# The weights' sums for the seven-product units on VectorE alone, without GpSimd

## The chip, the cores and the metric

One core of a Trainium2 chip. The metric is the device time of one execution in microseconds (us); the kernel before takes 732.95 us (median of 3 runs, 732.93 to 733.94). TensorE multiplies matrices (PE is its matmul, PEld its weight load), VectorE (DVE) and ScalarE (ACT) work element by element, GpSimd (POOL) does so too and issues the indirect gathers, SyncE (SP) issues most other transfers. Each engine takes its instructions in order; an instruction that waits for another engine holds up all that stand behind it on its own.

## The reference

Block-sparse attention and then a layer-normed feed-forward block, on q, k, v of 4 batches x 8 heads x 768 positions x 64. Cut to what matters:

```python
scores = scale * q @ k.T                      # per head; blocks of 32 positions
scores = where(mask, scores, -1e9)            # neighbours, first and last block, 3 sampled blocks
attn = softmax(scores) ; x = attn @ v         # x: (4, 768, 512)
xn = (x - mu) / sqrt(var + 1e-6) * g_ln
out = x + maximum(xn @ w_ch1, 0) @ w_ch2      # w_ch1: 512 x 2048, w_ch2: 2048 x 512
```

## The kernel before

The 768 positions of a batch are 6 tiles of 128, and 24 tiles in all. Attention goes in *visits*: a visit computes the scores of 4 or 8 heads of one tile (`scores`, L242), their maximum on VectorE (`biggest`, L286), softmax on ScalarE (`softmax`, L299), turns the weights with eight transposes on TensorE (`turn_pe`, L307), evicts those on ScalarE (`turn_act`, L310), and multiplies by the values (`attn_v`, L326), which VectorE scales (`evict`, L368 to L374). The finished tile is normed, and its transposed halves xt are made: GpSimd subtracts the high half from xn (`norm_5`, L423), and SyncE's queue turns both halves with transposing DMAs (L431, L432).

Two tiles are a unit of the feed-forward block. Weights and activations are held as pairs of fp16 tensors, a high and a low half; a product is three matmuls. Units 0 and 1 multiply plainly (`ffn_items`: L459 up, L468 and L471 the two halves after relu, L484 down, L435 the residual add, L439 the store). From unit 2 on (`wino_items`) the down product of two tiles and a 2 x 2 split of the second weight (B11, B12, B21, B22) is done with seven block products in place of eight: L564 is the up product, L571 its eviction by ScalarE into three buffers in turn (`con_s` the first), L572 to L574 the sums of activations, L583 and L584 their two halves, L589 the seven products. Three PSUM banks take the up products in turn, so TensorE can't begin the fourth group before L571 has emptied the first.

The seven products need four sums of weight blocks, S1 to S4, once. `combos` makes a list of them: the eight column slices go in four pairs, and for each pair 18 steps, each over 128 x 512 elements:

| step | engine before | what |
|---|---|---|
| 1, 2, 3 | GpSimd, VectorE, GpSimd | t = B12 + B22, high and low halves (L526) |
| 4, 5 | ScalarE, VectorE | S1 = -t, rounded to a high half (L521), and the rest as the low half (L522) |
| 6, 7, 8 | VectorE, GpSimd, VectorE | t = B11 - B12 (L526) |
| 9, 10 | ScalarE, VectorE | S3 |
| 11, 12 | GpSimd, VectorE | t = B22 - t (L526) |
| 13, 14 | ScalarE, VectorE | S2 |
| 15, 16 | GpSimd, VectorE | t = B21 - t (L526) |
| 17, 18 | ScalarE, VectorE | S4 |

t is one half of `con_s`, so two pairs run side by side; the list takes step 1 of one pair, step 1 of the other, step 2 of one, and so on, and then the same for the other two pairs: 72 entries, of which 20 are GpSimd's, 36 VectorE's and 16 ScalarE's.

From visit 13 on the list is emptied: 15 entries a visit, spread over the visit's other tasks (the gathers of values and the load of the next keys, `turn`, `norms`, and TensorE's share of the feed-forward block between them). So visits 13 to 16 take 15 each and visit 17 the last 12. Visit 16 begins in the second pair of pairs with the end of step 5, and visit 17 with step 13. Within a visit each engine's order is: `scores`, `biggest`, `attn_v` and `evict` of the visit before, `softmax`, and then the tasks. In visit 16 GpSimd's order is the store, three gathers and a sum, the fourth gather and a sum, L423, and a copy for the keys; SyncE's is L431, L432, then the keys and values of the visit after next (L190, L221, twelve of L196).

Scores start at 137.4 us in visit 13, 151.5 in visit 14, 165.3 in visit 15, and as the rows below show in visits 16, 17 and 18.

```python
for lo in range(0, NW, 2):                     # in combos
    t = con_s[:, 512 * (lo // 2 % 2) :][:, 0:512].rearrange("p (f e) -> p f e", e=256)
...
h = len(fns) // 4
return [f for k in (0, 2 * h) for x in zip(fns[k : k + h], fns[k + h : k + 2 * h]) for f in x]
...
if s == visits[NPV].job.visits[-1].i + 1:      # in the loop over visits, s = 13
    late.extend(combos())
k = min(15, len(late))
```

Of the kernel before, what the change touches and what calls it, by code (L numbers as in the profile page):

```python
# [14 lines left out]
ALU = mybir.AluOpType  # L15
# [10 lines left out]
def sparse_attention_moe(  # L26
# [19 lines left out]
    nc = tc.nc  # L46
# [460 lines left out]
    def block(w, r, c):  # L507
        return w[:, r * NW : r * NW + NW, 256 * c : 256 * c + 256]

    B11, B12, B21, B22 = ([block(w, r, c) for w in (w2h, w2l)] for r in range(2) for c in range(2))  # L510
# [6 lines left out]
    def combos():  # L517
        fns = []

        def rounded(t, dst, c, sign=1.0):  # L520
            fns.append(lambda: nc.scalar.activation(dst[0][:, c], t, AF.Copy, scale=sign))  # L521
            fns.append(lambda: nc.vector.scalar_tensor_tensor(out=dst[1][:, c], in0=t, scalar=sign, in1=dst[0][:, c],  # L522
                                                              op0=ALU.mult, op1=ALU.subtract))

        def op(eng, o, a, b, fn=ALU.add):
            fns.append(lambda: eng.tensor_tensor(out=o, in0=a, in1=b, op=fn))  # L526

        for lo in range(0, NW, 2):
            c = slice(lo, lo + 2)
            t = con_s[:, 512 * (lo // 2 % 2) :][:, 0:512].rearrange("p (f e) -> p f e", e=256)  # L530
            v, g = nc.vector, nc.gpsimd
            op(g, t, B12[0][:, c], B22[0][:, c])
            op(v, t, t, B12[1][:, c])
            op(g, t, t, B22[1][:, c])
            rounded(t, S1, c, -1.0)
            op(v, t, B11[0][:, c], B12[0][:, c], ALU.subtract)
            op(g, t, t, B11[1][:, c])
            op(v, t, t, B12[1][:, c], ALU.subtract)
            rounded(t, S3, c)
            for p, q in ((B22, S2), (B21, S4)):  # L540
                op(g, t, p[0][:, c], t, ALU.subtract)
                op(v, t, t, p[1][:, c])
                rounded(t, q, c)
        h = len(fns) // 4
        return [f for k in (0, 2 * h) for x in zip(fns[k : k + h], fns[k + h : k + 2 * h]) for f in x]
# [255 lines left out]
    def node(eng, cost, prio, fn, *args, after=(), dma=None, alloc=None, free=None, at=0.0, port=False):  # L801
        k = SimpleNamespace(eng=eng, cost=cost, prio=prio, fn=fn, args=args, dma=dma, alloc=alloc, free=free,
                            at=at, todo=0, next=[], start=None, must=True, port=port)
        for x in after:
            if x is not None:
                k.todo += 1
                x.next.append(k)
        nodes.append(k)
        return k
# [9 lines left out]
    for i in range(16):  # L819
# [15 lines left out]
        if LOWS[i] == "e":  # L835
            LO[i] = []
            for k in range(2):
                p = node("PE", 1.0, pr, low_pe, i, k, after=[HI[i]], alloc=(i, k))
# [133 lines left out]
    while left:  # L972
# [12 lines left out]
        while events and events[0][0] <= now + 1e-9:  # L985
            fn, args = heapq.heappop(events)[2:]
# [77 lines left out]
    while s < NV + LAG + 2 or queue or nextu < len(units):  # L1064
# [6 lines left out]
        if pvi:  # L1071
            t = pvi.tile
# [49 lines left out]
        if s == visits[NPV].job.visits[-1].i + 1:  # L1122
            late.extend(combos())
# [78 lines left out]
```

## Time and profile before

| | us |
|---|---|
| median of 3 runs | 732.95 |
| profiled execution | 739.73 |
| its span | 738.0 |
| TensorE busy in it | 696.5 (94%) |
| VectorE busy | 472.2 (64%) |
| GpSimd busy | 273.4 (37%) |

Time rows read: start in us, duration in us, engine, line, operation, output<-input, shapes and count; in brackets the idle time of the engine just before, and what ended it. Several instructions of one kind in a row are merged: "1.28 ... x2" is two in 1.28 us. An idle TensorE also shows as slow instructions, where a group waits between its members. The releaser named is the last event of those that the instruction waited for, by inference. "L242" is line 242 of the kernel printed above.

### The profile page before, as it was taken

The numbers are of one execution on the slowest core, as the hardware profiler recorded it, in microseconds if no ns is written. First come the engines' busy times: TensorE is split into PE (matmuls) and PEld (weight loads), VectorE is DVE, ScalarE is ACT, GpSimd is POOL, SyncE is SP. The second block draws the span as 40 slices with busy tenths as digits, with TensorE's granted clock in tenths as the row PEclk, the third lists the DMA queues.
The fourth block names the chain that finished last, engine by engine and source line by source line (L and its number), as shares of the span: only waits on it lengthen the run. The fifth ranks groups of instructions, "written<-read, shape, count | busy, mean of one in ns | idle before, by whom it ended". The sixth has DMA issues, their size and how long they took to land.

```text
span 738.0 us, 24907 instructions
## 1 busy us (share of the span) xinstructions
PE 696.5 (94%) x10258; PEld 553.1 (75%) x10258; DVE 472.2 (64%) x945; ACT 350.1 (47%) x668; POOL 273.4 (37%) x321
## 2 busy tenths in 40 slices
PE   2889988999879999999999999999999999999997
PEld 1466764675467888878888887788888878788886
DVE  4879986476577567558458468458458368448271
ACT  1577753453346455436446355336346355445150
POOL 3832732576655112435244113545353112520000
PEclk9999999999999999999999999999999999999999
DMA  8993861565367544677867554676678644750100
GB/s 332 411 391 142 289 201 56 151 167 161 90 192 219 159 163 139 170 188 217 197 189 226 176 161 117 181 237 190 175 212 193 198 141 119 179 163 16 44 1 30
DMA packets 127954, 128.83 MB, mean 175 GB/s; under 512 B 83681, under 2 KB 107745, under 8 KB 125153
## 3 DMA queue, kind: packets, MB, share of 16 engines
q1 hardware_dynamic: 117024, 92.09, 42.3%
q0 software_dynamic: 10528, 35.07, 15.2%
q8 instruction: 81, 1.33, 0.8%
q14 instruction: 33, 0.26, 0.1%
q10 hardware_dynamic: 288, 0.08, 0.0%
HBM read 115.40 MB, written 6.29 MB: 165 GB/s over the span
## 4 chain that ended last, share of the span: by engine, by line
PE 75%; DVE 10%; DMA 5%; issue 4%; SPq 2%; POOL 2%; ACT 0%; DVEq 0%; ACTq 0%; POOLq 0%
PE pu L564 26%; PE pd_X L589 10%; PE pd_Z L589 10%; PE ps L242 7%; PE pv L326 7%; PE pt L307 6%; PE pd_Y L589 3%; PE pu L459 3%; PE pd L484 2%; SPq L196 2%; DMA w2h<-w 2%; DVE st L286 1%; DVE con L526 1%; POOL con L526 1%; DMA ks<-kTh 1%
## 5 line engine op out<-in xcount | busy, mean ns | idle before, releaser
L227 POOL DMA_INDIRECT vs<-v,rows x152 | 161.4, 1062 | 219.3 <-PE pv L326 174.0
L564 PE MATMUL pu<-xt,w1h 128*128 128x256 f16 x1280 | 173.0, 273 | 3.0 <-DMA ks<-kTh 2.2
L299 ACT ACTIVATE p<-ps,st 128x256 f32<-128x256 f32 (+1 forms) x208 | 85.8, 490 | 119.3 <-DVE rs L368 44.6
L564 PEld LDWEIGHTS <-w1h 128*128 128x128 f16 x1280 | 123.9, 98 | 19.6 <-issue 3.4
L310 ACT COPY pt<-pt 128x512 f32<-128x512 f32 x120 | 61.4, 561 | 78.3 <-PE pt L307 31.6
L564 PE MATMUL pu<-xt,w1l 128*128 128x256 f16 x640 | 96.4, 273 | 0.0
L589 PEld LDWEIGHTS <-h 128*128 128x128 f16 x840 | 81.2, 98 | 11.8 <-issue 1.6
L286 DVE TENSOR_REDUCE st<-ps 128x4 f32<-128x1024 f32 (+1 forms) x60 | 68.9, 1149 | 32.2 <-PE ps L242 32.1
L326 PEld LDWEIGHTS pv<-vs,pt 128*32 128x32 f32 x3584 | 54.5, 109 | 31.5 <-issue 23.6
L242 PE MATMUL ps<-ks,q 64*32 64x256 f32 (+3 forms) x1952 | 71.4, 369 | 2.4 <-DMA ks<-kTh 1.3
L307 PE MATMUL pt<-id_sb,p 128*128 128x128 f32 x448 | 63.7, 281 | 10.1 <-ACT p L299 6.2
L326 PE MATMUL pv<-vs,pt 128*32 128x65 f32 x3584 | 65.8, 221 | 4.3 <-issue 3.5
L435 DVE SCALAR_TENSOR_TENSOR x<-pd_Z,x 128x256 f32<-128x256 f32 x40 | 16.1, 422 | 82.3 <-PE pd_Z L589 56.2
L564 PEld LDWEIGHTS <-w1l 128*128 128x128 f16 x640 | 62.3, 98 | 7.6
L307 PEld LDWEIGHTS pt<-id_sb,p 128*128 128x128 f32 x448 | 51.1, 143 | 18.6 <-ACT p L299 10.3
L242 PEld LDWEIGHTS ps<-ks,q 64*32 64x32 f32 x1952 | 33.4, 107 | 24.0 <-issue 15.3
L589 PEld LDWEIGHTS <-stg 128*128 128x128 f16 x420 | 40.4, 98 | 6.5 <-issue 0.9
L423 POOL TENSOR_TENSOR xl<-xn,xh 128x512 f16<-128x512 f32 x21 | 24.4, 1162 | 41.9 <-ACT xh L400 41.6
L439 POOL DMA_DIRECT2D out<-x x20 | 11.7, 587 | 73.6 <-DVE x L435 67.7
L484 PE MATMUL pd<-w2h,h 128*128 128x512 f16 x128 | 38.4, 379 | 0.0
L572 DVE TENSOR_TENSOR con<-con 128x256 f32<-128x256 f32 x30 | 12.8, 427 | 38.5 <-ACT con L571 33.9
L459 PE MATMUL pu<-xt,w1h 128*128 128x256 f16 x256 | 35.4, 273 | 0.0
(181 smaller groups left out, 1171.5 us busy)
## 6 DMA issues: line engine op xcount, KB each, us to landing
vs<-vN SPq DMA_DIRECT2D x35, 520.0 KB
ks<-kNh SPq DMA_DIRECT2D x32, 512.0 KB
ks<-kTh SPq DMA_DIRECT2D x384, 32.0 KB
q<-qT SPq DMA_DIRECT2D x24, 256.0 KB
w2h<-w SPq DMA_DIRECT2D x5, 1024.0 KB
out<-x POOLq DMA_DIRECT2D x20, 256.0 KB
vs<-vD SPq DMA_DIRECT2D x6, 780.0 KB
ks<-kTh SPq DMA_DIRECT2D x12, 384.0 KB
```

What stands on the lines that cost most here:

```text
L227: nc.gpsimd.indirect_dma_start(out=vj.buf[:, vj.far + gg, :], out_offset=None, in_=src, in_offset=bass.IndirectOffsetOnAxis(ap=rows[:, i : ...
L242: nc.tensor.matmul(ps[32 * part : 32 * part + 32, col : col + n], lhs[64 * row : 64 * row + 64], rhs[64 * row : 64 * row + 64], start=True ...
L286: nc.vector.tensor_reduce(out=st[:, 0:n], in_=seen(vi), axis=AX.X, op=ALU.max, negate=True)
L299: nc.scalar.activation(p_s[:, h * w : (h + 1) * w], seen(vi)[:, h, :], AF.Exp, bias=vi.st[:, 4 + h : 5 + h], scale=0.125)
L307: nc.tensor.transpose(pt[:, k - lo, :], p_s[:, k * P : (k + 1) * P], id_sb)
L310: nc.scalar.copy(pt_s[:, lo:hi, :], vi.pt.pop(lo)[:, 0 : hi - lo, :])
L326: nc.tensor.matmul(pv[32 * row : 32 * row + 32, 65 * col : 65 * col + 65], pt[:, ch, 32 * row : 32 * row + 32], vj.buf[:, vv, lo : lo + 65 ...
L423: nc.gpsimd.tensor_sub(xl_s[t.n % 2], xn_s, xh_s[t.n % 2])
L459: nc.tensor.matmul(ph[:, j * n : (j + 1) * n], w[:, ct, fs], x[:, ct, 0:n], start=m == 0, stop=m == 3 * CT - 1, skip_group_check=True)
L484: nc.tensor.matmul(po, x[:, f, ts], w[:, f, :], start=m + f == 0, stop=m == 2 and f == FT - 1)
L564: nc.tensor.matmul(ph[:, j * 256 : j * 256 + 256], w[:, ct, f * P : (f + 1) * P], x[:, ct, :], start=m == 0, stop=m == 3 * CT - 1, skip_gr ...
L589: nc.tensor.matmul(o, HW[j][x][:, i, :], t[w][:, j, :], start=first and m + j == 0, stop=False, skip_group_check=True)
```

## The change

The 20 sums that GpSimd made (steps 1, 3, 7, 11 and 15 of each pair) become VectorE's, in the same place of the list. Operands, buffers, the number of entries and where they are put in the visits stay as they are. ScalarE's 16 roundings stay.

```diff
--- before.py
+++ after.py
@@ -522,24 +522,23 @@
             fns.append(lambda: nc.vector.scalar_tensor_tensor(out=dst[1][:, c], in0=t, scalar=sign, in1=dst[0][:, c],
                                                               op0=ALU.mult, op1=ALU.subtract))
 
-        def op(eng, o, a, b, fn=ALU.add):
-            fns.append(lambda: eng.tensor_tensor(out=o, in0=a, in1=b, op=fn))
+        def op(o, a, b, fn=ALU.add):
+            fns.append(lambda: nc.vector.tensor_tensor(out=o, in0=a, in1=b, op=fn))
 
         for lo in range(0, NW, 2):
             c = slice(lo, lo + 2)
             t = con_s[:, 512 * (lo // 2 % 2) :][:, 0:512].rearrange("p (f e) -> p f e", e=256)
-            v, g = nc.vector, nc.gpsimd
-            op(g, t, B12[0][:, c], B22[0][:, c])
-            op(v, t, t, B12[1][:, c])
-            op(g, t, t, B22[1][:, c])
+            op(t, B12[0][:, c], B22[0][:, c])
+            op(t, t, B12[1][:, c])
+            op(t, t, B22[1][:, c])
             rounded(t, S1, c, -1.0)
-            op(v, t, B11[0][:, c], B12[0][:, c], ALU.subtract)
-            op(g, t, t, B11[1][:, c])
-            op(v, t, t, B12[1][:, c], ALU.subtract)
+            op(t, B11[0][:, c], B12[0][:, c], ALU.subtract)
+            op(t, t, B11[1][:, c])
+            op(t, t, B12[1][:, c], ALU.subtract)
             rounded(t, S3, c)
             for p, q in ((B22, S2), (B21, S4)):
-                op(g, t, p[0][:, c], t, ALU.subtract)
-                op(v, t, t, p[1][:, c])
+                op(t, p[0][:, c], t, ALU.subtract)
+                op(t, t, p[1][:, c])
                 rounded(t, q, c)
         h = len(fns) // 4
         return [f for k in (0, 2 * h) for x in zip(fns[k : k + h], fns[k + h : k + 2 * h]) for f in x]
```

## Rows read from the trace of the kernel before

**Rows 1.** The page's part 4: chain that ended last, shares of the span

```profile
PE 75%; DVE 10%; DMA 5%; issue 4%; SPq 2%; POOL 2%; ACT 0%; DVEq 0%; ACTq 0%; POOLq 0%
```

**Rows 2.** Busy time by stretch: engines busy (operations), granted clock, DMA share, GB/s

```profile
135.00:215.00 80.00, 72.84 (x905) 49.62 (x903) 49.16 (x78) 30.91 (x66) 52.46 (x50) 0.98 0.59 167
205.00:210.00 5.00, 4.21 (x26) 3.61 (x27) 2.64 (x7) 2.60 (x6) 2.47 (x4) 0.66 0.71 187
240.00:720.00 480.00, 476.47 (x7079) 401.12 (x7078) 294.85 (x649) 229.41 (x438) 148.00 (x161) 1.00 0.57 159
```

**Rows 3.** TensorE's timeline, 130 to 225 us: start, duration, [idle before <-releaser]

```profile
145.57 1.04 PE L307 MATMUL pt<-id_sb,p 128*128 128x128 f32 x8
...
158.57 1.53 PE L307 MATMUL pt<-id_sb,p 128*128 128x128 f32 x8 [0.29 <-issue]
...
180.97 1.09 PE L242 MATMUL ps<-ks,q 64*32 64x256 f32 x32
...
187.37 1.53 PE L307 MATMUL pt<-id_sb,p 128*128 128x128 f32 x8 [1.12 <-ACT p L299]
...
192.28 1.09 PE L242 MATMUL ps<-ks,q 64*32 64x256 f32 x32
...
200.89 1.03 PE L564 MATMUL pu<-xt,w1h 128*128 128x256 f16 x8 [0.79 <-DMA xt<-xl]
...
205.79 1.97 PE L307 MATMUL pt<-id_sb,p 128*128 128x128 f32 x8 [3.21 <-issue]
...
207.55 1.40 PE L564 MATMUL pu<-xt,w1h 128*128 128x256 f16 x6
...
216.00 0.38 PE L564 MATMUL pu<-xt,w1h 128*128 128x256 f16 x2 [2.25 <-DMA ks<-kTh]
...
216.31 1.34 PE L242 MATMUL ps<-ks,q 64*32 64x256 f32 x32
```

**Rows 4.** Groups by line, 134 to 222 us: busy us, mean ns | idle before

```profile
L526 DVE TENSOR_TENSOR con<-con,w2l 128x512 f32<-128x512 f32 x16 | 16.0, 1024 | 13.3 <-POOL con L526 13.3
...
L526 POOL TENSOR_TENSOR con<-w2h,con 128x512 f32<-128x512 f16 x8 | 10.6, 1345 | 5.6 <-DVE vs L522 4.0 <-ACT pt L310 1.6
```

**Rows 5.** VectorE's timeline, same stretch and columns

```profile
178.53 2.57 DVE L526 TENSOR_TENSOR con<-con,w2l 128x512 f32<-128x512 f32 x2 [1.43 <-POOL con L526]
...
182.82 0.98 DVE L522 SCALAR_TENSOR_TENSOR ks<-con,ks 128x512 f16<-128x512 f32 x1 [1.72 <-ACT ks L521]
...
185.32 1.22 DVE L286 TENSOR_REDUCE st<-ps 128x4 f32<-128x1024 f32 x1
...
188.60 1.28 DVE L526 TENSOR_TENSOR con<-w2h 128x512 f32<-128x512 f16 x2
...
194.60 0.69 DVE L526 TENSOR_TENSOR con<-con,w2l 128x512 f32<-128x512 f32 x1 [4.72 <-POOL con L526]
...
203.58 1.21 DVE L286 TENSOR_REDUCE st<-ps 128x4 f32<-128x1024 f32 x1
...
207.38 1.29 DVE L522 SCALAR_TENSOR_TENSOR vs<-con,vs 128x512 f16<-128x512 f32 x2 [1.54 <-issue]
```

**Rows 6.** GpSimd's timeline, same stretch and columns

```profile
192.43 0.95 POOL L227 DMA_INDIRECT vs<-v,rows  x1 [0.30 <-issue]
...
193.40 1.16 POOL L526 TENSOR_TENSOR con<-con,w2l 128x512 f32<-128x512 f32 x1
...
197.25 1.16 POOL L423 TENSOR_TENSOR xl<-xn,xh 128x512 f16<-128x512 f32 x1
...
220.38 1.65 POOL L227 DMA_INDIRECT vs<-v,rows  x1 [0.30 <-issue]
```

**Rows 7.** ScalarE's timeline, same stretch and columns

```profile
215.34 0.61 ACT L571 ACTIVATE con<-pu 128x512 f32<-128x512 f32 x1
```

**Rows 8.** SyncE's DMA queue, same columns: duration is that of the issue

```profile
198.44 1.19 SPq L432 DMA_TRANSPOSE xt<-xl  x1
...
200.93 6.68 SPq L196 DMA_DIRECT2D ks<-kTh  x12
```

## The prediction

> **What bounds the kernel now.** I read four views in this order: the chain of waits, the busy time by stretch, the timeline of the stretch in which the sums run, and the timelines of the queues behind it. The chain is three quarters TensorE [rows 1], and from 240 to 720 us TensorE is busy 476.47 of 480 us at the full granted clock [rows 2]: what is saved or lost before 240 moves the rest as a block. The sums run between about 134 and 215 us (visits 13 to 17). From 135 to 215 TensorE loses 80 - 72.84 = 7.2 us, while VectorE is busy only 49.16 of 80 [rows 2]. So I ask of each TensorE gap there which engine ended it, and whether the sums stood in that engine's queue.
>
> They do. VectorE's 16 low-half sums wait 13.3 us for GpSimd and take 1024 ns each, because they run beside GpSimd's own sums, which take 1345 ns [rows 4]. The same VectorE pair takes 1.28 us for two when GpSimd is not summing (188.60), but 2.57 when it is (178.53) [rows 5]. In order behind it stands the maximum of the scores (L286): in visit 17 the scores were done by 193.4 [rows 3], yet L286 starts at 203.58 [rows 5], since VectorE sat 4.72 us for a GpSimd sum that stood behind gathers [rows 5, 6]. TensorE's transposes need softmax, and start 2.1 to 2.2 us after L286 starts [rows 3, 5].
>
> **The gaps, and what each costs.** A normal group of eight transposes takes 1.04 us [rows 3].
> - G1, 158.57: 0.29 idle and 0.49 slow (1.53 against 1.04).
> - G2, 187.37: 1.12 idle, 0.49 slow.
> - G3, 200.89: 0.79 idle for xt, whose low half GpSimd (L423) makes behind two sums [rows 3, 6].
> - G4, 205.79: 3.21 idle; then transposes 0.93 slow and the next matmuls some 0.6 slow (six in 1.40; eight take 1.03 at 200.89, so six some 0.8), as the granted clock fell to 0.66 of full in that stretch, so part of it at the lower of its two levels (1.2 against 2.4 GHz) [rows 2, 3]. In all 4.7.
> - G5, 216.00: 2.25 idle, then scores 0.25 slow (1.34 against 1.09). The view names a key load, but TensorE starts just as ScalarE's eviction at L571 ends (215.34 + 0.61) [rows 3, 7]; ScalarE came to it only after steps 17, which waited for sums.
>
> **The change part by part.** It removes 20 GpSimd sums, adds 20 to VectorE, and moves nothing else; the order on each engine stays. *Price of a moved sum:* 0.64 us, half of the pair of 1.28, since the steps of two column blocks alternate. Bounds: below, no gain beyond 0.64 is shown; above, 1.29, half of the disturbed pair of 2.57 [rows 5]. I take 0.64: the cause of the 1.29, a GpSimd sum alongside, goes. So VectorE gets 20 x 0.64 = 12.8 us, and loses 16 x (1.024 - 0.64) = 6.1 of disturbance and 13.3 of waiting [rows 4]. It would be busy 49.2 - 6.1 + 12.8 = 56 of 80: it fits. *GpSimd* loses some 20 x 1.3 = 26 us; nothing waits for that but its gathers, stores and L423, which come earlier.
>
> What the same queues give, visit by visit:
> - Visit 14: two more sums (step 7, 1.3) stand ahead of L286, but waits and disturbance go, on average (13.3 + 6.1) / 5 = 3.9 a visit. More than G1 asks for; it gives 0.7 (estimate: the idle and most of the slow part).
> - Visit 15 to 16: VectorE waited 1.43 before 178.53 and 1.72 before 182.82, and was disturbed by 1.29 in the pair and 0.3 in step 5 [rows 5]: 4.7 less. Steps 1 and 3 add 4 x 0.64 = 2.6. L286 moves from 185.32 to about 183.2, after the scores of visit 16 (done by 182.1 [rows 3], 0.7 earlier by G1). G2's idle goes: 1.1; the slow part I leave.
> - Visit 17: from L286 of visit 16 to 188.60 is 3.3 [rows 5], so step 6 starts at 186.5; steps 6, 7, 8, 10, 11 and 12 are 12 operations, 7.7, and a hand-over to ScalarE some 0.2. L286 comes at 194.4, 9 us earlier; transposes could start at 196.6. TensorE gets there at (205.79 - 3.21) - 0.7 - 1.1 - 0.8 = 200.0: cover 3.4. G4 gives 4.7.
> - G3: L423 stands behind four gathers and the store; that chain starts when VectorE ends the residual add just ahead of 188.60 [rows 5], which moves by 2.1, and loses the two sums of 1.16 [rows 6] and pauses of some 0.2: L423 from 197.25 to 192.6. G3 gives 0.8.
> - G5: after L286 of visit 17 step 14 follows in 3.8 (before, 203.58 to 207.38, by the softmax), then steps 14, 15, 16 and a residual add, 7 x 0.64 = 4.5; ScalarE's step 17, two evictions of transposes and L571 are four operations, at L571's 0.61 [rows 7] another 2.4: 194.4 + 3.8 + 4.5 + 2.4 = 205.1. TensorE wants it at (216.00 - 2.25) - 7.3 = 206.4. Cover 1.3, the thinnest; G5 gives 2.5.
>
> Sum: 0.7 + 1.1 + 0.8 + 4.7 + 2.5 = 9.8 us.
>
> **What is late next.** The key loads of visit 18 leave SyncE behind L432 (198.44), which waits for L423; they are issued by 207.6 [rows 8]. No row shows when they land; the nearest is the transpose DMA: 198.44 to TensorE's start at 200.89, 2.45 [rows 3, 8]. With L423 4.6 earlier they are usable at 207.6 - 4.6 + 2.45 = 205.5. TensorE wants them at 216.31 - 9.6 = 206.7. Cover 1.2, so this costs nothing, but only just.
>
> The profiled execution took 739.73 (span 738.0), 6.8 over the median 732.95; I take the 9.8 from either: span 728.2, median 723.2.
>
> **The rivals.**
> *A, GpSimd's queue gains less than I think.* A gather that starts at 220.38 takes 1.65 instead of 0.95 [rows 6]. If a busier VectorE does that to all four, L423 loses 2.8, the keys come at 208.3 and TensorE waits 1.6: 724.8. If L423 does not move at all, keys come at 207.6 + 2.45 = 210.1, 3.4 late, and the clock may fall again for the 1.5 it cost in G4: gain 9.8 - 4.9, 728.0. For it: the cover is 1.2. Against: the gathers at 192 take 0.95 [rows 6], though VectorE was idle then.
> The Trainium skill ("SBUF — State Buffer", section "Who interferes with whom") says that a VectorE instruction with two SBUF inputs contends with a GpSimd instruction that reads SBUF, and infers that descriptor generation, which needs the write interface, is left alone by tensor_tensor. By that the gathers would stay at 0.95 and A would cost nothing; the 1.65 row leaves it open.
> *B, VectorE becomes the engine waited for.* At 1.29 a sum, L286 of visit 16 comes at 183.2 + 4 x 0.65 = 185.8: G2 stays and grows by 0.5. L286 of visit 17 comes at 199.6 and costs little; L571 is 10 x 0.65 = 6.5 later, 211.6, so TensorE goes on 4.4 earlier than now, and 0.25 of slow scores goes: gain about 4.6, 728.3.
> The Trainium skill ("Perfetto Trace Analysis", section "Optimizing Scalar/DVE Operations") says that where VectorE is saturated, moving work to GpSimd may make sense. That speaks for the kernel as it is, with B's result; VectorE's 49.16 of 80 says that the condition is not met.
> *C, slower: a moved sum waits out a gather.* Place: visits 16 and 17, where gathers and sums now run together. The fall comes back when L571 is 10.9 us later than I have it (205.1 to 216.0), ten sums before it: from 0.64 + 1.09 = 1.73 us a sum. With a gather of 0.95 and a half of a second, a sum takes 2.0; L571 is 13.6 later, 218.7: 2.7 slower, 735.6. For it: VectorE's sums did double beside GpSimd's. Against: gathers take 0.95 to 1.65 each and there are four a visit, not one for each sum.
> *D, no change:* the gain is given back by key loads later. Against: after 240 TensorE waits 3.5 us in all [rows 2].
>
> **How the numbers follow.** My forecast 0.65 (721.5 to 724.5: the slow halves of G1 and G2 add up to 0.6, the thin covers take 1.3), A 0.15, B 0.08, D 0.05, C 0.07. Forecast, A and B are faster: 0.88; same 0.05; slower 0.07; 0.2% (1.5 us) is about what a measurement of this kernel can tell. The range reaches from 720.5 (less by the 0.6, by 0.5 of gaps before 215 that I did not count, by as much again just after 216, and by the 1.0 that runs of the kernel before differ) to 728.5 (A and B in), leaving C and D out.
>
> **What would show it.** Right: all 40 sums (L526) on VectorE, near 0.64 each; no VectorE wait for GpSimd; L286 of visit 17 near 194; no granted clock below full at 205; L423 near 193; TensorE over 79 of 80 busy in the stretch; the stretch after 240 alike, moved by 10 us. Wrong: TensorE waiting for key loads at visit 18 (A), or L286 and ScalarE's evictions still late with VectorE near full (B, C).

## The result, and the profile after

The changed kernel takes 721.97 us (median of 5; before 732.95, median of 5): ratio 0.9845, 95% interval 0.9825 to 0.9865, 11.0 us faster. The forecast was 723.2 with 9.8 us. One execution of the 5 took 1415.92 us, with matmuls of 442 ns where the others of this study have 273, and is left out of the ratio; it was the one that was profiled, so the trace below is of the same kernel, run once more (719.21 us).

The opening stage differs from execution to execution by several us: the scores of visit 13 begin at 137.40 in the trace of before, at 131.90 in this one, and between 131.5 and 140.2 in the others. The stretch behind differs too: from the scores of visit 19 to the end it is 507.2 us in the trace of before, 503.4 in this one, and 502.7 to 508.1 in the others. So the time of one trace is not compared with that of another; traces are laid beside one another from visit to visit, from the start of one visit's scores to the next. All in us:

| kernel | 13 | 14 | 15 | 16 | 17 | 18 | 13 to 18 |
|---|---|---|---|---|---|---|---|
| before | 14.05 | 13.82 | 15.70 | 11.31 | 24.03 | 14.51 | 93.42 |
| changed | 13.63 | 12.87 | 15.70 | 9.53 | 15.75 | 14.59 | 82.07 |

The 0.42 of visit 13 is of that one execution of before: kernels with the old sums in visit 13 have 13.62 too (the last pairs, below). The rest, 10.9 us, is the change, about what the medians give (11.0), and it sits where the gaps were: 0.95 in visit 14 (G1), 1.78 in visit 16 (G2), 8.28 in visit 17 (G3 to G5).

Busy time by stretch (columns as in rows 2), first before, from the scores of visit 13 to those of visit 18, then the changed kernel over the same work and after it:

```profile
137.40:216.31 78.91, 70.75 (x893) 48.44 (x892) 49.70 (x79) 30.67 (x64) 50.23 (x48) 0.98 0.59 169
```

```profile
131.90:199.38 67.48, 67.11 (x892) 47.50 (x891) 56.79 (x99) 30.82 (x64) 26.98 (x28) 1.00 0.62 176
226.00:700.00 474.00, 472.65 (x7054) 399.10 (x7053) 290.52 (x642) 226.56 (x432) 147.48 (x161) 1.00 0.58 162
```

TensorE does the same matmuls in 67.48 us instead of 78.91 (busy 70.75 before, the slow ones among them, and 67.11 now), and its granted clock is 1.00, against 0.98 before. VectorE has 7.1 us more to do (the forecast: 12.8 - 6.1 = 6.7) in a stretch that is 11 us shorter, so it is busy 84% of it and not 63%.

TensorE's timeline of the changed kernel (columns as in rows 3; lines behind the edit have a number one lower than before, and in the runs with added lines one that is some higher):

```profile
145.53 1.09 PE L242 MATMUL ps<-ks,q 64*32 64x256 f32 x32
...
152.19 1.04 PE L307 MATMUL pt<-id_sb,p 128*128 128x128 f32 x8
...
158.40 1.09 PE L242 MATMUL ps<-ks,q 64*32 64x256 f32 x32
...
174.10 1.09 PE L242 MATMUL ps<-ks,q 64*32 64x256 f32 x32
...
179.21 1.04 PE L307 MATMUL pt<-id_sb,p 128*128 128x128 f32 x8
...
183.63 1.09 PE L242 MATMUL ps<-ks,q 64*32 64x256 f32 x32
...
190.69 1.04 PE L563 MATMUL pu<-xt,w1h 128*128 128x256 f16 x8
...
192.22 1.04 PE L307 MATMUL pt<-id_sb,p 128*128 128x128 f32 x8
...
199.08 0.38 PE L563 MATMUL pu<-xt,w1h 128*128 128x256 f16 x2 [0.37 <-ACT con L570]
199.38 1.37 PE L242 MATMUL ps<-ks,q 64*32 64x256 f32 x32
...
207.93 1.53 PE L307 MATMUL pt<-id_sb,p 128*128 128x128 f32 x8 [0.78 <-ACT p L299]
```

Of the gaps, G1 to G4 have no successor: the transposes of visits 14, 16 and 17 (152.19, 179.21, 192.22) take the normal 1.04 without a wait, and so does the up product that waited for xt (190.69). Of G5 0.37 is left (199.08), the scores behind it are slow as before, and the wait of visit 18 (207.93) is one that the kernel before has too (0.73 us at 224.77 in its trace). VectorE's, GpSimd's and ScalarE's timelines of the changed kernel:

```profile
180.87 2.49 DVE L526 TENSOR_TENSOR con<-con,w2l 128x512 f32<-128x512 f32 x4
...
185.87 2.69 DVE L526 TENSOR_TENSOR con<-con,w2l 128x512 f32<-128x512 f32 x2
188.49 1.21 DVE L286 TENSOR_REDUCE st<-ps 128x4 f32<-128x1024 f32 x1
```

```profile
180.95 1.46 POOL L227 DMA_INDIRECT vs<-v,rows  x1 [0.30 <-issue]
182.72 1.47 POOL L227 DMA_INDIRECT vs<-v,rows  x1 [0.30 <-issue]
...
186.84 1.16 POOL L423 TENSOR_TENSOR xl<-xn,xh 128x512 f16<-128x512 f32 x1
```

```profile
198.42 0.61 ACT L570 ACTIVATE con<-pu 128x512 f32<-128x512 f32 x1
```

Four sums in a row take 2.49 us (180.87), 0.62 each, and no sum waits for another engine. Counted from the scores of visit 13, L286 of visit 17 comes at 56.6 instead of 66.2 [rows 5], L423 at 54.9 instead of 59.9 [rows 6], L571 (now L570) at 66.5 instead of 77.9 [rows 7]; the 0.42 of visit 13 is in each of these differences. But the pair at 185.87 takes 2.69, beside L423, which reads too; and the two gathers at 180.95 and 182.72, beside the sums, take 1.46 and not 0.95: what rival A named does occur.

The sums by form, 128 to 215 us of the changed kernel (columns as in rows 4):

```profile
L526 DVE TENSOR_TENSOR con<-con,w2l 128x512 f32<-128x512 f32 x24 | 17.3, 770 | 0.0
...
L526 DVE TENSOR_TENSOR con<-w2h,con 128x512 f32<-128x512 f16 x8 | 5.4, 706 | 0.0
...
L526 DVE TENSOR_TENSOR con<-w2h 128x512 f32<-128x512 f16 x8 | 5.1, 682 | 0.0
```

Against 1024 ns and a wait of 13.3 us [rows 4], the mean is 0.68 to 0.77 us and the wait is none.

### The profile page after: what moved, and what is told of

Read it like the earlier page. It is cut to its first block, busy times and chain, and to the rows that moved or that the text cites. A ratio compares the mean times of both kernels' runs of the same rounds, so it can differ in the third digit from the quotient of the medians.

```text
span 1414.2 us, 24904 instructions
## 1 busy us (share of the span) xinstructions
PE 1397.7 (99%) x10258; PEld 846.3 (60%) x10258; DVE 478.4 (34%) x965; ACT 359.6 (25%) x668; POOL 238.3 (17%) x301
## 4 chain that ended last, share of the span: by engine, by line
PE 99%; DMA 1%; ACT 0%; DVE 0%; DVEq 0%; issue 0%
PE pu L563 32%; PE pd_X L588 12%; PE pd_Z L588 12%; PE ps L242 8%; PE pv L326 8%; PE pt L307 7%; PE pu L459 6%; PE pd L484 6%; PE pd_Y L588 4%; PE pw L716 2%; DMA id_sb<-eye 1%; PE pw L717 1%; PE idle L796 0%; PE px L408 0%; PE px L416 0%; ACT w1l L722 0%
## 5 line engine op out<-in xcount | busy, mean ns | idle before, releaser
L563 PE MATMUL pu<-xt,w1h 128*128 128x256 f16 x1280 | 337.5, 442 | 0.0
L563 PEld LDWEIGHTS <-w1h 128*128 128x128 f16 x1280 | 185.1, 146 | 108.8 <-issue 4.7
L563 PE MATMUL pu<-xt,w1l 128*128 128x256 f16 x640 | 183.2, 447 | 0.0
L588 PEld LDWEIGHTS <-h 128*128 128x128 f16 x840 | 124.4, 149 | 69.1 <-issue 2.2
L286 DVE TENSOR_REDUCE st<-ps 128x4 f32<-128x1024 f32 (+1 forms) x60 | 69.2, 1153 | 210.9 <-PE ps L242 210.8
L326 PEld LDWEIGHTS pv<-vs,pt 128*32 128x32 f32 x3584 | 96.2, 147 | 54.4 <-issue 35.2
L307 PE MATMUL pt<-id_sb,p 128*128 128x128 f32 x448 | 117.4, 446 | 1.1 <-ACT p L299 1.1
L242 PE MATMUL ps<-ks,q 64*32 64x256 f32 (+3 forms) x1952 | 115.2, 611 | 0.0
L326 PE MATMUL pv<-vs,pt 128*32 128x65 f32 x3584 | 112.7, 318 | 0.0
L484 PE MATMUL pd<-w2h,h 128*128 128x512 f16 x128 | 72.8, 675 | 0.0
L459 PE MATMUL pu<-xt,w1h 128*128 128x256 f16 x256 | 68.4, 432 | 0.0
L484 PEld LDWEIGHTS <-h 128*128 128x128 f16 x192 | 27.5, 146 | 53.9 <-issue 52.3
L571 DVE TENSOR_TENSOR con<-con 128x256 f32<-128x256 f32 x30 | 13.5, 450 | 127.6 <-ACT con L570 127.6
L588 PE MATMUL pd_X<-w2h,h 128*128 128x256 f16 x160 | 54.6, 454 | 0.0
```

The costliest lines, as they stand in the source:

```text
L242: nc.tensor.matmul(ps[32 * part : 32 * part + 32, col : col + n], lhs[64 * row : 64 * row + 64], rhs[64 * row : 64 * row + 64], start=True ...
L286: nc.vector.tensor_reduce(out=st[:, 0:n], in_=seen(vi), axis=AX.X, op=ALU.max, negate=True)
L307: nc.tensor.transpose(pt[:, k - lo, :], p_s[:, k * P : (k + 1) * P], id_sb)
L326: nc.tensor.matmul(pv[32 * row : 32 * row + 32, 65 * col : 65 * col + 65], pt[:, ch, 32 * row : 32 * row + 32], vj.buf[:, vv, lo : lo + 65 ...
L459: nc.tensor.matmul(ph[:, j * n : (j + 1) * n], w[:, ct, fs], x[:, ct, 0:n], start=m == 0, stop=m == 3 * CT - 1, skip_group_check=True)
L484: nc.tensor.matmul(po, x[:, f, ts], w[:, f, :], start=m + f == 0, stop=m == 2 and f == FT - 1)
```

## The experiments

Two questions: where the gain sits (by visits), and which of the two things that went together was the loss, the waits of VectorE and GpSimd for one another's results, or the disturbance of a VectorE operation by a GpSimd operation that runs beside it. Times by visit stand in one table at the end of this section.

**The changed kernel again.** No edit.

> The changed kernel once more, for a trace that can be laid beside that of the kernel before. The forecast's theory: all gaps G1 to G5 go because VectorE no longer hands sums back and forth with GpSimd. Then a span near 720 to 728, the maximum of visit 17 (L286) near 194 us, L423 near 193, no TensorE wait over 1 us and no fallen clock between 155 and 220 us, and the stretch behind 240 us the same but for a shift of about 10. Rival A: TensorE waits 1.5 us or more ahead of the scores of visit 18, for keys. Rival B: a sum on VectorE takes well over 0.64 us and a wait for VectorE or ScalarE is left.

Measured 719.27 (5 runs; before on the same chip 732.12): 0.984 (0.9817 to 0.9863). The trace is the one above: the forecast's theory holds, A's wait is not there, and of B's there is only the 0.37 for L570. The span of 717.4 is below the 720 that I gave, by the shorter opening.

**The first pairs, the last pairs.**

```diff
-            v, g = nc.vector, nc.gpsimd
+            v, g = nc.vector, nc.vector if lo < 4 else nc.gpsimd      # first; last: lo >= 4
```

> Only the first two of the four column pairs (visits 13, 14 and the start of 15) are summed without GpSimd, the other two as before. The forecast's theory: the gap G1 alone lies behind those, so 0.7 us is gained, about 732. A rival, that every sum taken off GpSimd gives its share wherever it stands (less contention, a shorter queue): half of the 11 us measured, about 727.5.

> Only the last two column pairs (end of visit 15, visits 16 and 17) are summed without GpSimd. The forecast's theory: G2 to G5 go, 9.1 of 9.8 us, so within 1 us of the changed kernel, about 722.7. The rival of equal shares: about 727.5.

Measured 730.21, 0.9974 (0.9955 to 0.9993), and 721.54, 0.9846 (0.9821 to 0.9871). The shares are not equal: ten sums in visits 13 to 15 are worth 1.9 us, the other ten 10.6. By visits the first pairs give 0.95 in visit 14 and 0.5 in visit 16, the last pairs all of 1.78 in visit 16 and 8.15 in visit 17. The first pairs give more than my 0.7: visit 14 gives G1's idle, its slow part and some 0.2 more, and the 0.5 of visit 16 was not in the forecast. With the last pairs alone G1 is there as before (0.28 idle).

**Idle sums on GpSimd.** The changed kernel, and in the old places a sum that nobody needs (the edit is made in the kernel before, where `op` is still told the engine; `...` stands for lines left out):

```diff
...
+                if eng is nc.gpsimd:
+                    n = spare.pop(0)
+                    nc.gpsimd.tensor_tensor(out=extra[:, n % 4], in0=B12[0][:, 0:2], in1=B22[0][:, 0:2], op=fn)
+                nc.vector.tensor_tensor(out=o, in0=a, in1=b, op=fn)
...
```

> The changed kernel, and GpSimd makes 20 sums besides, in the places where it made them before, into a buffer that nobody reads: its queue and its reads of the memory are as busy as before, but no engine waits for a result. If the waits for GpSimd's results were the loss: most of the gain stays, 722 to 724. If the disturbance was (VectorE's sums at 1.0 to 1.3 us beside GpSimd's), rival B's sum: about 728. If GpSimd's queue was (L423 and the keys behind it late): TensorE waits for xt and for the keys of visit 18, 725 to 728, and the trace names those waits.

Measured 739.84, 1.0117 (1.0088 to 1.0146): slower than every case that I had written down, and slower than the kernel before, though nobody waits for a result of these 20 sums. VectorE's and GpSimd's timelines, then TensorE's:

```profile
142.21 4.94 DVE L523 SCALAR_TENSOR_TENSOR ks<-con,ks 128x512 f16<-128x512 f32 x1 [1.30 <-ACT ks L522]
...
158.49 2.39 DVE L523 SCALAR_TENSOR_TENSOR vs<-con,vs 128x512 f16<-128x512 f32 x2
...
170.88 5.21 DVE L287 TENSOR_SCALAR st<-st 128x4 f32<-128x4 f32 x1
```

```profile
141.76 2.26 POOL L532 TENSOR_TENSOR stg<-w2h 128x512 f32<-128x512 f16 x2
143.97 0.39 POOL L207 COPY ks<-kg 128x256 f32<-128x256 f32 x1
144.34 2.27 POOL L532 TENSOR_TENSOR stg<-w2h 128x512 f32<-128x512 f16 x2
...
157.62 4.27 POOL L532 TENSOR_TENSOR stg<-w2h 128x512 f32<-128x512 f16 x3
...
171.25 1.17 POOL L532 TENSOR_TENSOR stg<-w2h 128x512 f32<-128x512 f16 x1
172.34 0.41 POOL L207 COPY ks<-kg 128x256 f32<-128x256 f32 x1
172.70 3.36 POOL L532 TENSOR_TENSOR stg<-w2h 128x512 f32<-128x512 f16 x3
```

```profile
155.28 1.53 PE L307 MATMUL pt<-id_sb,p 128*128 128x128 f32 x8 [2.69 <-ACT p L299]
...
176.74 1.97 PE L307 MATMUL pt<-id_sb,p 128*128 128x128 f32 x8 [4.57 <-ACT p L299]
...
216.79 0.58 PE L572 MATMUL pu<-xt,w1h 128*128 128x256 f16 x2 [4.38 <-ACT con L579]
```

A rounding of 0.69 us takes 4.94 (142.21), and goes on until GpSimd's five operations (141.76 to 146.61) are through; a scaling of four numbers a partition, 0.17 us elsewhere, takes 5.21 (170.88) and ends with GpSimd's run (171.25 to 176.06). In these two places it is not one GpSimd operation that VectorE waits out, but all that stand in a row. It is not so in every place: beside the three sums that begin at 157.62 VectorE ends two roundings in 2.39 (158.49) and then a sum, and there it is GpSimd that is slow, 4.27 for three. No run shows what decides between the two. The TensorE waits of 2.69, 4.57 and 4.38 are in the visits 14, 15 and 17 that are long in the table. So the disturbance, with a wait of 0.97 for xt in visit 17 as the share of GpSimd's own queue, can cost more than the whole gain (visits 13 to 18 are 18.2 us longer than in the changed kernel). It does not say how much of the loss of before it was: with nothing to wait for, these sums run in longer rows than the old ones did.

**Fills instead of sums.** The kernel before, with GpSimd's order and all its waits, but writing without reading; two fills for each sum, then three:

```diff
...
+                if eng is nc.gpsimd:
+                    nc.gpsimd.memset(extra[:, 0], 0.0)
+                    nc.gpsimd.memset(extra[:, 1], 0.0)      # the run with three only
+                    nc.gpsimd.memset(o, 0.0)
+                    return
...
```

> The kernel before, but each of GpSimd's 20 sums is two fills with zero, the first into a buffer that nobody reads and the second into the place of the sum (so the sums' values are left out). The order on every engine and all waits between VectorE and GpSimd are those of the kernel before; what goes is that GpSimd reads the memory while VectorE does. If the hand-over in turn (two queues in order, each held by the other's work) was the loss: about the time of the kernel before, 729 to 734, with VectorE's 4 to 5 us wait for GpSimd in visit 16 still there. If the disturbance of VectorE's two-input operations was: 720 to 725. Both a part: between.

> As the kernel whose GpSimd sums were two fills each (sums' values left out), but with three fills: at 0.47 us from one to the next about 1.5 us for each sum, longer than GpSimd's sums of the kernel before (1.16 to 1.35). It tells whether the time came back because GpSimd did not read or only because two fills are shorter. If reading was the loss: visits 13 to 16 stay as in the changed kernel, and only visit 17, where the waits in turn are, is longer by about 1 to 3 us than with two fills; 725 to 728. If the length was: 732 or more, with the gaps of visits 14 and 16 back.

Measured with two fills 724.88, 0.9899 (0.9865 to 0.9932); with three 734.61 on a chip that gives the kernel before 737.95, 0.995 (0.9928 to 0.9971). VectorE's and TensorE's timelines with two fills, and then with three, there with GpSimd's between them:

```profile
183.96 0.69 DVE L533 TENSOR_TENSOR con<-con,w2l 128x512 f32<-128x512 f32 x1 [4.52 <-POOL con L531]
```

```profile
178.78 1.04 PE L307 MATMUL pt<-id_sb,p 128*128 128x128 f32 x8
...
193.20 1.53 PE L307 MATMUL pt<-id_sb,p 128*128 128x128 f32 x8 [1.25 <-ACT p L299]
...
202.57 0.38 PE L572 MATMUL pu<-xt,w1h 128*128 128x256 f16 x2 [2.38 <-ACT con L579]
```

```profile
192.87 0.69 DVE L534 TENSOR_TENSOR con<-con,w2l 128x512 f32<-128x512 f32 x1 [4.99 <-POOL con L532]
```

```profile
165.33 0.52 POOL L530 MEMSET stg<- 128x512 f32 x1
165.80 0.52 POOL L531 MEMSET stg<- 128x512 f32 x1
168.70 0.52 POOL L532 MEMSET con<- 128x512 f32 x1 [2.38 <-DVE vs L522]
```

```profile
187.22 1.04 PE L307 MATMUL pt<-id_sb,p 128*128 128x128 f32 x8
...
203.31 1.97 PE L307 MATMUL pt<-id_sb,p 128*128 128x128 f32 x8 [2.19 <-ACT p L299]
...
213.62 0.38 PE L573 MATMUL pu<-xt,w1h 128*128 128x256 f16 x2 [2.16 <-ACT con L580]
```

VectorE's long wait in visit 16 is there, 4.52 and 4.99 (before: 4.72 [rows 5]), and TensorE waits in visit 17 at two of the old places, the transposes and the eviction of the up product. By the ranges that I had written down 724.88 is at the edge of the case of disturbance (720 to 725); the visits show a part of each. G1 and G2 are gone whatever the length of the fills: visit 14 takes 12.88 and 13.20 (the changed kernel in two traces: 12.87 and 13.19), visit 16 takes 9.53 in all of them. The order stayed, and so did VectorE's waits late in visit 15: they were 3.15 in the kernel before (1.43 and 1.72 [rows 5]) and are 3.27 with three fills. What went is the disturbance: the pair and the rounding of [rows 5] took 3.55 and take 2.24, 1.3 less where G2 waited 1.12; ahead of G1 a sum that took 1.63 (153.09 in the trace of before) takes 0.68 (154.59), 0.95 less where G1 waited 0.29. That covers both gaps, so their 2.7 us are put down to GpSimd's reading. It is not shown to be the reading alone, since the fills differ from the sums in one thing more: where GpSimd waits for VectorE, all fills of a sum but the last run ahead of the wait, and behind it one of 0.52 is enough (168.70), where a sum took its whole time:

```profile
169.35 2.60 POOL L526 TENSOR_TENSOR con<-w2h,con 128x512 f32<-128x512 f16 x2 [3.34 <-DVE vs L522]
```

This row is of the kernel before, at the same place in visit 15. The hand-over behind a wait is thus shorter as well, three times ahead of G2.

Visit 17 goes with the length: 19.68 at two fills (0.99 us a sum, from the starts of fills 0.47 apart and a last one of 0.53), 22.29 at three (1.46). GpSimd's sums took 1.16 to 1.35 [rows 4, 6], which on that line is 20.6 to 21.7: of the 8.28 us that visit 17 lost, some 4.9 to 5.9 are the waits in turn, the other 2.4 to 3.4 disturbance. By visits 17 and 18 together the waits come out the same to 0.1. That last split is worked out along a straight line between two runs, and not measured by itself. My expectation for three fills (725 to 728) missed by its own scale, since that chip is 5 us slower; against the kernel before it is 3.7 us faster, where I had 5 to 8.

**Twice on VectorE.** The changed kernel with a second sum into a spare buffer (again as an edit of the kernel before):

```diff
...
+                if eng is nc.gpsimd:
+                    n = spare.pop(0)
+                    nc.vector.tensor_tensor(out=extra[:, n % 4], in0=B12[0][:, 0:2], in1=B22[0][:, 0:2], op=fn)
+                nc.vector.tensor_tensor(out=o, in0=a, in1=b, op=fn)
...
```

> The changed kernel, and VectorE makes each of the 20 moved sums twice, the second time into a buffer that nobody reads: a moved sum costs about 1.28 us instead of 0.64, and GpSimd stays idle beside it. Rival B's sum for just that price: 4.6 us of the gain are left, about 728 where the kernel before is 732.9. If VectorE has more cover than the forecast thinks (a summing visit is longer on TensorE than its VectorE work): within 2 us of the changed kernel. If it has less: slower than the kernel before.

Measured 732.72, 0.9997 (0.9977 to 1.0017): all of the gain is gone, not half. Busy time from the scores of visit 13 to those of visit 18, and TensorE's waits:

```profile
131.56:209.29 77.73, 70.34 (x893) 47.58 (x892) 69.58 (x119) 30.65 (x64) 32.77 (x28) 1.00 0.54 157
```

```profile
152.68 1.53 PE L307 MATMUL pt<-id_sb,p 128*128 128x128 f32 x8 [0.67 <-ACT p L299]
...
169.89 1.53 PE L307 MATMUL pt<-id_sb,p 128*128 128x128 f32 x8 [1.43 <-ACT p L299]
...
208.98 0.38 PE L572 MATMUL pu<-xt,w1h 128*128 128x256 f16 x2 [2.68 <-ACT con L579]
```

12.8 us more VectorE work (56.79 to 69.58) lengthen the stretch by 10.3 us. The rival's price was worked out at L286 of two visits and at L571; the waits of 0.67 and 1.43 for softmax in visits 14 and 15 (152.68, 169.89) were not in it. These visits are 1.65 and 2.42 longer than in the changed kernel, 4.1 of the 4.4 by which the price was wrong.

**A late xt.** The changed kernel with five fills ahead of L423 in visit 16.

```diff
+    con_x = stg.bitcast(F32)
...
     def norm_5(t):
+        if t.n == 5:
+            for i in range(5):
+                nc.gpsimd.memset(con_x[:, 512 * (i % 4) :][:, 0:512], 0.0)
         nc.gpsimd.tensor_sub(xl_s[t.n % 2], xn_s, xh_s[t.n % 2])
```

> The changed kernel with five fills ahead of L423 in visit 16 on GpSimd, some 2.5 us: xt's low half and, behind it on SyncE's queue, the keys of visit 18 come that much later. Nothing else waits for them. Rival A's mechanism by itself. The forecast had a cover of 1.2 us for the keys; by the trace of the changed kernel xt has a cover of only 0.2. So a TensorE wait of about 2 us for xt ahead of the second up product of the first seven-product unit, and about 2 us on the whole. If GpSimd's queue does not matter there: no change from the changed kernel.

Measured 721.91, 0.986 (0.981 to 0.9911), which can't be told from the changed kernel. TensorE's timeline, its weight load, and then VectorE's and GpSimd's:

```profile
194.37 1.03 PE L568 MATMUL pu<-xt,w1h 128*128 128x256 f16 x8 [1.98 <-DMA xt<-xl]
...
202.54 1.61 PE L242 MATMUL ps<-ks,q 64*32 64x256 f32 x32
...
210.38 1.04 PE L307 MATMUL pt<-id_sb,p 128*128 128x128 f32 x8
```

```profile
203.10 0.57 PEld L242 LDWEIGHTS ps<-ks,q 64*32 64x32 f32 x20 [0.39 <-DMA ks<-kTh]
```

```profile
189.93 2.00 DVE L287 TENSOR_SCALAR st<-st 128x4 f32<-128x4 f32 x1
```

```profile
188.38 2.40 POOL L427 MEMSET stg<- 128x512 f32 x5
190.74 1.16 POOL L428 TENSOR_TENSOR xl<-xn,xh 128x512 f16<-128x512 f32 x1
```

The wait for xt is there and of the size foreseen, 1.98. But it is given back: the 0.37 at the eviction and the 0.78 at the next transposes are gone, as VectorE and ScalarE meanwhile went on, and over visits 13 to 18 it costs 0.4. A wait for keys shows only in the weight load: 0.39 in the middle of visit 18's scores (203.10), which take 1.61 instead of 1.37. So rival A's mechanism is real, for xt and for the keys, and at 2.4 us it costs next to nothing on the whole. The fills did one thing more that was not meant: the scaling L287 of visit 17 begins beside them and ends only with L423 behind them (here L428), 2.00 us for 0.17.

**Two tries at more.** Sixteen entries a visit; and L423 on VectorE, beside a third run of the changed kernel on the same chip.

```diff
-        k = min(15, len(late))
+        k = min(16, len(late))
...
-        nc.gpsimd.tensor_sub(xl_s[t.n % 2], xn_s, xh_s[t.n % 2])
+        nc.vector.tensor_sub(xl_s[t.n % 2], xn_s, xh_s[t.n % 2])
```

> The changed kernel with 16 entries of the list a visit instead of 15, so that visit 17 has 8 left and not 12. It tells how much cover VectorE has in visits 14 to 17. If there is 0.6 us more in each: the rest of the wait at L571 in visit 17 (0.4 us) goes and nothing comes back, 0 to 0.5 us faster than the changed kernel. If visit 17's maximum is at its limit: slower than it by about 0.6 to 2 us.

> The changed kernel with L423 (the low half of xt) on VectorE too, for all tiles: GpSimd makes no more two-input operation. If a reading GpSimd holds VectorE up wherever it runs: the pair of sums beside L423 in visit 16 (2.69 us in the changed kernel) falls to 1.3, L286 of visit 17 comes about 0.7 earlier in spite of the 0.6 that L423 costs VectorE, the wait of 0.4 at L571 goes, keys leave earlier; 0 to 2 us faster than the changed kernel. If VectorE is at its limit: slower by up to 2.

> The changed kernel beside the run with L423 on VectorE, on the same chip, to compare these two directly: 719 to 722.5.

Sixteen: 720.44, 0.9823 (0.9797 to 0.9848); L423 on VectorE: 725.35, 0.9822 (0.9797 to 0.9848); the changed kernel beside the latter: 726.96, 0.9856 (0.9832 to 0.9879). All intervals overlap with the changed kernel's, so neither is shown to be faster. The third run missed its range of 719 to 722.5 because that chip is slower, before and after alike. L423 on VectorE did not do what I had written down for it: the pair of 2.69 falls to 1.68 and not to 1.3, and L286 of visit 17 comes no earlier (4.67 us after its visit's scores, 4.63 in the third run). In the stretch itself sixteen saves 1.85 us, above the 0 to 0.5 of its expectation: its visits 13 to 16 are 0.3 to 0.6 longer each, visit 17 2.3 and visit 18 1.7 shorter.

Visits of all runs, us:

| kernel | 13 | 14 | 15 | 16 | 17 | 18 | 13 to 18 |
|---|---|---|---|---|---|---|---|
| first pairs | 13.62 | 12.87 | 15.71 | 10.82 | 24.04 | 14.50 | 91.56 |
| last pairs | 13.62 | 13.81 | 15.71 | 9.53 | 15.88 | 14.59 | 83.14 |
| idle sums on GpSimd | 13.61 | 17.65 | 23.05 | 9.53 | 21.32 | 15.16 | 100.32 |
| two fills | 13.62 | 12.88 | 15.70 | 9.53 | 19.68 | 14.66 | 86.07 |
| three fills | 14.46 | 13.20 | 15.70 | 9.53 | 22.29 | 14.50 | 89.68 |
| twice on VectorE | 13.62 | 14.52 | 18.12 | 11.74 | 19.73 | 14.59 | 92.32 |
| late xt | 13.61 | 12.88 | 15.70 | 9.53 | 17.36 | 13.39 | 82.47 |
| sixteen a visit | 13.94 | 13.40 | 16.34 | 10.17 | 13.50 | 12.87 | 80.22 |
| L423 on VectorE | 13.62 | 13.17 | 15.70 | 9.52 | 17.72 | 12.87 | 82.60 |
| changed, third run | 13.62 | 13.19 | 15.71 | 9.52 | 17.14 | 12.97 | 82.15 |

Visits 17 and 18 of the changed kernel are 15.75 and 14.59 in one trace, 17.14 and 12.97 in another; their sum is the same to 0.3, so it is the sums that count.

## Why the prediction was right

- *The stage.* Right: the gain is in visits 14, 16 and 17, and what was won by visit 18 stays. From 226 to 700 us the changed kernel's TensorE loses 1.4 of 474 us; the kernel before lost 3.5 of 480 [rows 2], and how much is lost there differs among traces of one kernel (2.6 of 474 in the changed kernel's third run).
- *The price of a moved sum.* 0.64 forecast; 0.62 in an undisturbed row of four, 0.68 to 0.77 as a mean with the pair beside L423 in it. Twenty sums more (twice on VectorE) add 12.8 us, 0.64 each. The two pairs from which the price was read, 188.60 and 178.53, are not the same in form as the prediction has it (the first has fp16 inputs alone); one of the second's form takes 1.28 too when GpSimd is not summing (172.62 in the trace of before), so the price stands. VectorE's net work: 6.7 forecast, 7.1 measured.
- *G1 to G5.* Forecast 0.7, 1.1, and 8.0 for G3 to G5 together; measured 0.95, 1.78 and 8.28. G1 and G2 were sized too low by 0.9 in all: I had left G2's slow transposes where they were, and they went. G5 kept 0.37 of its wait and the slow scores, some 0.6 in all, against a forecast that gave it whole; the rest of visit 17 gave 0.9 more than its sum, of which 0.33 is a TensorE wait ahead of the values' product (194.06 in the trace of before) that I had not counted. These three, 0.9 - 0.6 + 0.9, are the 1.2 by which the gain exceeds the forecast. Without the 0.42 of visit 13, L286 of visit 17 came 9.2 earlier (forecast 9.2), L423 4.5 (4.6), L571 11.0 (10.9).
- *G1's queue* was counted short: not two moved sums but six, steps 1, 3 and 7, stand ahead of L286 of visit 14, 3.8 us and not 1.3. It did no harm, since VectorE had idled 5.1 us there in the kernel before (1.5 now), and since the 0.7 was read from the gap and not from the queue.
- *What ended the gaps.* I counted waits (13.3 us) and disturbance (6.1) as one parcel that goes away together. It did, so the sum held; but the fills show that they sit in different places: G1 and G2 go when GpSimd no longer reads, though VectorE still waits, and visit 17 for the larger part with the waits (by the straight line above). Of VectorE's own time the disturbance took 4.6 us (49.70 busy before, 45.1 with fills), where I had 6.1.
- *"It fits", 56 of 80.* The load was right, the stretch was not: TensorE does the same work in 67.48 us, so VectorE is at 84%. TensorE's shorter stretch was the gain itself, and I had left it out of the division. This is the step that went wrong without harm to the sum. Twice the price costs the whole gain (732.72) where rival B, at nearly the same price, had 728.3: B left out the softmax of visits 14 and 15.
- *Rival A.* The lengthened gathers came (1.46 for 0.95), and the keys and xt were in time nevertheless; made 2.4 us later, both were waited for, at a cost of 0.4. The Trainium skill ("SBUF — State Buffer", section "Who interferes with whom") infers that tensor_tensor leaves descriptor generation alone; the measurement decides: gathers beside the sums take 1.46 and 1.47, half as much again. No run says whether it is the reading or the writing of the gather that is held up.
- *Rival C* needed a moved sum to be held up by a gather. Four sums ran in 2.49 us beside those gathers: it is the gather that is lengthened, not the sums.

## What to carry to other kernels

Before work is put on GpSimd to relieve VectorE, look at what stands behind the hand-over in VectorE's queue: here 20 sums on an engine with time to spare held up the maximum of the scores, then softmax, then TensorE. And count what GpSimd's reading costs VectorE where nobody waits for its result; fills in its place cost VectorE's sums next to nothing here. Once an engine has been given the work, take its share of the shorter stretch, not of the old one, to say how much more it can bear.

## What the runs showed of the hardware that was not expected

- A VectorE operation that meets GpSimd two-input operations in a row can be held up until the whole row is through: 4.94 us for a rounding of 0.69, 5.21 for a scaling of 128 x 4 numbers that takes 0.17, each over four sums and a copy. It need not be: beside three sums in a row (157.62 of the same trace) two roundings and a sum were ended. The Trainium skill ("SBUF — State Buffer", section "Who interferes with whom") has the second engine blocked until the first one's instruction ends; in the first two places here it was blocked over five.
- GpSimd fills of 128 x 512 (0.51 to 0.55 us, 0.47 from one to the next) did not do that to VectorE's sums and roundings: with 40 or 60 of them in place of the sums VectorE was busy 45.1 us from the scores of visit 13 to those of visit 18, against 49.70 with GpSimd's sums. They are not harmless to all its operations: a scaling of 0.17 that began beside five fills took 2.00, to the end of the subtraction behind them (the run with a late xt).
- A delay of 2 us ahead of TensorE cost 0.4 by the end of the next visit, as the engines behind it used the time: a TensorE wait that is followed by waits for other engines is not lost one for one.
